# One ReLU moves from ScalarE to VectorE in a fused cluster attention and MLP kernel

## The chip, the cores and the metric

The kernel runs on one core of a Trainium2 chip. The metric is the device time of one execution in microseconds (us). A core has five engines that run their own instruction queues in order and wait for each other by semaphores: TensorE (PE in the profile, its weight loads are PEld), VectorE (DVE), ScalarE (ACT), GpSimd (POOL) and SyncE (SP), which here only issues transfers. Matmul results land in PSUM; everything else lives in SBUF.

## The reference

Queries, keys and values have shape (4 batches, 8 heads, 768 positions, 64). Each query and key is put into one of 16 clusters, a query attends to the keys of its own cluster, and the result (3072 tokens of 512) goes through an MLP with an inner layer of 2048:

```python
q_assign = np.argmax(np.einsum('bhsd,hcd->bhsc', q_n, c_n), axis=-1)
k_assign = np.argmax(np.einsum('bhsd,hcd->bhsc', k_n, c_n), axis=-1)
mask = q_assign[:, :, :, None] == k_assign[:, :, None, :]
scores = np.where(mask, scale * np.matmul(q, k.transpose(0, 1, 3, 2)), -1000000000.0)
attn = softmax(scores)            # max taken off, 1e-9 added to the sum
x = (attn @ v).transpose(0, 2, 1, 3).reshape(3072, 512)
h = x @ w_in
r = np.maximum(h, 0.0)
g = s * (r * r) + b
out = g @ w_out
```

## The kernel before

Products are taken in float16 with a high and a low part of each operand, so that three matmuls stand for one.

**Attention.** A *unit* is one (batch, query chunk, head pair, query tile of 128, head); there are 192. Query chunks are two tiles, 256 positions. For a unit, PE makes the scores `sc` (128 x 768, L456), DVE takes the row maximum (L465, `ssm`), ACT turns it into a bias (L472) and takes the exponential out of PSUM (L475, `p`), ACT writes the float16 high part `ph` (L119, in a few units DVE, L121), POOL the low part (L498), a transposing DMA turns both (L500, `PT`), and PE multiplies by the values into `px` (L517 to L519). DVE scales the result into `xs` (L525, L526, L529), and for each four units it is split, turned and put down as `x` (L540 to L546). Scores have two PSUM buffers.

**MLP.** A *step* is one (batch, query chunk, block `ft` of 128 inner columns); there are 12 x 16 = 192, named `r_b_c_ft`, `h_b_c_ft` and `g_b_c_ft` for batch, chunk and block. A step makes `h` (128 x 256 in one PSUM bank, 12 matmuls, L575), then takes the ReLU times a factor `cf` out of PSUM into `r` (L582), squares `r` into the float16 high part `g` (L584) and in place (L585), POOL subtracts the two for the low part of `g` (L590), and PE adds the step to the output sums `acc` (6 matmuls, L602). `cf` is one number per partition, made on DVE from the largest absolute value of the chunk's `x` (L560 to L564). There is one `h` bank (`ps_h`, bufs=1), so the `h` matmuls of a step wait until the ReLU of the step before has read it. `r` has two buffers, `g` four.

**Preparation.** For each batch and chunk, Q, K and V are loaded (L85, from SyncE's queue, behind the last transpose issued before), DVE takes their largest absolute value (L101: `amb_q`, `amb_k`, `vm`), PE and DVE spread it over the partitions (L97, L98), ACT and DVE split into high and low parts (L185, L187), and the cluster one-hot is made (L288 to L294). The weights are read once, narrowed ahead of the first step (L203 to L223), and split (L267, L269) while the first steps run.

**Order.** The main loop runs over units; step `m` is written `LAG` = 21 units behind. One pass writes scores, the output of step `m - 2`, the maximum and exponential, then `mlp_in` and `mlp_relu` of step `m`, then the low parts, values and one piece of each preparation at work. This is only a priority: the framework's scheduler then places each instruction on its engine's queue by its own estimate of times, so that a change of one instruction's engine can move others on all queues. On the chip each queue runs in the order so fixed.

## Time and profile before

| what | value |
|---|---|
| median of 3 runs | 986.11 us (985.94 to 988.25) |
| profiled execution | span 986.0 us, from its first to its last instruction |
| mean granted TensorE clock | 0.941 of full |
| PE / PEld busy | 834.3 us (85%) / 580.2 us (59%) |
| ACT busy | 726.4 us (74%), 1416 instructions |
| DVE busy | 673.0 us (68%), 1475 instructions |
| POOL busy | 550.2 us (56%) |
| the ReLU, L582 on ACT | 192 instructions, 89.1 us busy, 464 ns each |
| first and last ReLU | start at 179.0 and 977.8 us |

Only the span is given for the profiled execution, no time of its own beside it; it lies within the range of the runs. Busy time is a sum over stages with different limits; PE's busy time includes pipelining, so it says less than what PE waits for. In rows of groups the columns are: line, engine, operation, output and inputs with shapes, count, then total busy us, mean ns of one, then the engine's idle time just before them and what ended it. In rows of the timeline: start in us, duration in us, engine, line, operation, tiles, and in brackets the idle time before it and its releaser. In rows of waits: who waited, for whom, total us, number of times, the longest.

### The profile page before, as it was taken

The page shows a single profiled execution, that of the slowest core. Times are in us where ns is not written, and L with a number is a line of the kernel's source. Part 1 is how long each engine was busy: PE and PEld are TensorE (multiplying, and loading weights), DVE is VectorE, ACT ScalarE, POOL GpSimd, SP SyncE. Part 2 cuts the span into 40 slices and gives each one's busy share as a digit, 9 for nine tenths or more (in the row PEclk, how much of TensorE's full clock was granted, in tenths as well). Part 3 has the DMA queues.
Part 4 walks back from the last instruction along what each step waited for, and adds up shares of the span by engine and source line. Part 5 has one row for each costly group of instructions (what it writes and reads, how often), then busy time and mean ns, then how long its engine had stood idle before and what let it go on. Part 6 is the DMA issues. An engine that isn't in the chain of part 4 may idle for free. (4 is left out here: it accounts for less than half of the span.)

```text
span 986.0 us, 22497 instructions
## 1 busy us (share of the span) xinstructions
PE 834.3 (85%) x8625; PEld 580.2 (59%) x8625; DVE 673.0 (68%) x1475; ACT 726.4 (74%) x1416; POOL 550.2 (56%) x543
## 2 busy tenths in 40 slices
PE   0568524887899999998799999997889999999997
PEld 0347312654566666765566666765666666767764
DVE  7798889989687665658787756578867567473100
ACT  4476776877578788867678877876788977789443
POOL 3125755556456576655467656655566766667322
PEclk9955566999999999999999999999999999999999
DMA  6865883687678775698888767797888676777200
GB/s 181 204 196 158 222 210 90 138 194 134 128 144 163 156 161 123 140 210 154 171 164 156 169 132 156 138 203 181 138 160 173 151 119 142 142 138 149 44 23 21
DMA packets 450299, 147.36 MB, mean 149 GB/s; under 512 B 417936, under 2 KB 446608, under 8 KB 450192
## 3 DMA queue, kind: packets, MB, share of 16 engines
q1 hardware_dynamic: 450192, 145.93, 69.7%
q8 instruction: 67, 1.10, 0.5%
q14 instruction: 40, 0.33, 0.1%
HBM read 35.69 MB, written 6.29 MB: 43 GB/s over the span
## 5 line engine op out<-in xcount | busy, mean ns | idle before, releaser
L498 POOL TENSOR_TENSOR ph<-p,ph 128x768 f16<-128x768 f32 x184 | 308.6, 1677 | 170.7 <-ACT ph L119 135.8
L575 PE MATMUL h<-x,wis 128*128 128x256 f16 x2304 | 292.0, 275 | 17.3 <-ACT r L582 12.2
L602 PE MATMUL acc<-wos,g 128*128 128x512 f16 x1152 | 295.4, 380 | 4.7 <-POOL g L590 2.9
L575 PEld LDWEIGHTS <-wis 128*128 128x128 f16 x2304 | 223.1, 98 | 74.9 <-issue 16.6
L590 POOL TENSOR_TENSOR g<-r,g 128x256 f16<-128x256 f32 x192 | 133.3, 695 | 139.7 <-ACT r L585 129.8
L465 DVE TENSOR_REDUCE ssm<-sc 128x1 f32<-128x768 f32 x192 | 180.9, 950 | 16.2 <-PE sc L456 16.0
L475 ACT ACTIVATE p<-sc,ssm,qsm 128x768 f32<-128x768 f32 x192 | 188.1, 980 | 3.9 <-DMA PT<-ph 1.8
L602 PEld LDWEIGHTS <-g 128*128 128x128 f16 x1152 | 104.1, 98 | 88.2 <-POOL g L590 6.9
L119 ACT ACTIVATE ph<-p 128x768 f16<-128x768 f32 x174 | 144.8, 832 | 11.1 <-DMA PT<-ph 10.8
L472 ACT ACTIVATE ssm<-ssm,lift,qsm 128x1 f32<-128x1 f32 x192 | 73.4, 382 | 101.9 <-DVE ssm L465 101.4
L517 PE MATMUL px<-vh,PT 128*128 128x65 f16 x1104 | 119.9, 196 | 14.5 <-DVE ksm L98 5.2
L582 ACT ACTIVATE r<-h,cf 128x256 f32<-128x256 f32 x192 | 89.1, 464 | 55.0 <-PE h L575 50.8
L518 PE MATMUL px<-vl,PT 128*128 128x64 f16 x1104 | 119.9, 193 | 0.0
L519 PE MATMUL px<-vh,PT 128*128 128x65 f16 x1104 | 119.9, 194 | 0.0
L456 PE MATMUL sc<-KA,QA 128*128 128x384 f16 x384 | 101.1, 343 | 20.2 <-ACT p L475 16.9
L518 PEld LDWEIGHTS <-PT 128*128 128x128 f16 x1104 | 103.6, 100 | 21.2 <-issue 12.8
L517 PEld LDWEIGHTS <-PT 128*128 128x128 f16 x1104 | 103.9, 98 | 17.5 <-issue 9.1
L456 PE MATMUL sc<-KB,QB 128*128 128x384 f16 x384 | 100.2, 345 | 7.8 <-DMA QB<-qb 7.7
L519 PEld LDWEIGHTS <-PT 128*128 128x128 f16 x1104 | 103.6, 98 | 3.0
L584 ACT ACTIVATE g<-r 128x256 f16<-128x256 f32 x192 | 79.5, 414 | 3.8
L585 ACT ACTIVATE r<-r 128x256 f32<-128x256 f32 x192 | 79.1, 412 | 3.3
L525 DVE TENSOR_SCALAR ssm<-px 128x2 f32<-128x2 f32 x92 | 14.2, 155 | 88.3 <-PE px L519 88.2
(153 smaller groups left out, 1090.9 us busy)
## 6 DMA issues: line engine op xcount, KB each, us to landing
wst<-in_moe_w_in_dram SPq DMA_DIRECT2D x16, 512.0 KB, 4.5
wst<-in_moe_w_out_dram SPq DMA_DIRECT2D x16, 512.0 KB, 4.1
kn<-in_k_dram SPq DMA_DIRECT2D x16, 384.0 KB, 3.9
qn<-in_q_dram SPq DMA_DIRECT2D x24, 256.0 KB, 3.8
vn<-in_v_dram SPq DMA_DIRECT2D x16, 384.0 KB, 4.4
out_dram<-o SPq DMA_DIRECT2D x12, 512.0 KB, 3.2
PT<-ph SPq DMA_TRANSPOSE x184, 3.4
x<-xn SPq DMA_TRANSPOSE x48, 2.5
```

Of the source, the lines that this page charges most:

```text
L119: A.activation(dst, src, AF.Copy)
L456: last_score[0] = nc.tensor.matmul(sc[:, e, :HALF], X[:, col, :], y[:, h * S + e * HALF : h * S + (e + 1) * HALF], start=st, stop=not st)
L465: last_max[0] = V.tensor_reduce(SM[i // 4][:, 0, j : j + 1], U[i]["sc"], axis=AX.XY, op=ALU.max, negate=True)
L475: last_exp[0] = A.activation(p.rearrange("p (a b) -> p a b", a=2), u["sc"], AF.Exp, bias=bi, scale=u["scale"], **total)
L498: G.tensor_tensor(u["ph"][:, 1, :], u["p"], u["ph"][:, 0, :], op=ALU.subtract)
L517: nc.tensor.matmul(o1, PT[:, kt, :], vh[:, h, kt, : D + 1], start=(kt == 0), stop=False)
L518: nc.tensor.matmul(o, PT[:, kt, :], vl[:, h, kt, :], start=False, stop=False)
L519: nc.tensor.matmul(o1, PT[:, T + kt, :], vh[:, h, kt, : D + 1], start=False, stop=(kt == T - 1))
L575: nc.tensor.matmul(ph[:, :CW], WSP[ft][0][:, wl, kt, :], XS[(b, c, kt)][:, :, xl, :], start=(i == 0), stop=(i == len(terms) - 1))
L582: A.activation(r, ph[:, :CW], AF.Relu, scale=MS[(b, c)][0])
L590: G.tensor_tensor(g[:, 1, :], r, g[:, 0, :], op=ALU.subtract)
L602: nc.tensor.matmul(acc[:, t, :], g[:, gl, rows], WSP[ft][1][:, wl, :], start=(ft == 0 and gl + wl == 0), stop=(ft == NF - 1 and gl == 1))
```

## The change

The ReLU with its factor leaves ACT and becomes one VectorE instruction with two scalars: first the maximum of `h` and 0, then the product with `cf`. `cf` is positive, so that max(h, 0) x cf is what ACT computed as max(cf x h, 0). Both squares stay on ACT.

```diff
@@ -579,7 +579,7 @@
         n = f"{b}_{c}_{ft}"
         ph = GS[(b, c, ft)]
         r = sb.tile([P, CW], F32, tag="r", name=f"r_{n}", bufs=2)
-        A.activation(r, ph[:, :CW], AF.Relu, scale=MS[(b, c)][0])
+        V.tensor_scalar(r, ph[:, :CW], 0.0, MS[(b, c)][0], op0=ALU.max, op1=ALU.mult)
         g = sb.tile([P, 2, CW], F16, tag="g", name=f"g_{n}", bufs=4)
         A.activation(g[:, 0, :], r, AF.Square)
         A.activation(r, r, AF.Square)
```

The scheduler places the rest anew from the first ReLU on. DVE's queue around the preparation of the queries `qn_2_1_0` (batch 2, chunk 1, first four heads), which falls into the first steps of batch 1, chunk 2, before the change:

```order
L465 TENSOR_REDUCE ssm_100_7675<-sc_103_7870 128x1
L525 TENSOR_SCALAR ssm_96_7406<-px_96_7779 128x2
L465 TENSOR_REDUCE ssm_104_7970<-sc_104_7957 128x1
L526 RECIPROCAL ssm_96_7406<-ssm_96_7406 128x2
L529 TENSOR_TENSOR xs_24_7818<-px_96_7779,ssm_96_7406 128x128
L101 TENSOR_REDUCE amb_q2_1_0_7951<-qn_2_1_0_7868 128x2
L525 TENSOR_SCALAR ssm_96_7406<-px_98_7910 128x2
L526 RECIPROCAL ssm_96_7406<-ssm_96_7406 128x2
L529 TENSOR_TENSOR xs_24_7818<-px_98_7910,ssm_96_7406 128x128
```

The same place of DVE's queue with the change:

```order
L529 TENSOR_TENSOR xs_24_7818<-px_96_7779,ssm_96_7406 128x128
L582 TENSOR_SCALAR r_1_2_0_7770<-h_1_2_0_7757,cf_1_2_7753 128x256
L566 SCALAR_TENSOR_TENSOR xm_20_6746<-xm_20_6746,glob_130 128x1
L101 TENSOR_REDUCE amb_q2_1_0_7951<-qn_2_1_0_7868 128x2
L582 TENSOR_SCALAR r_1_2_1_7859<-h_1_2_1_7846,cf_1_2_7753 128x256
L525 TENSOR_SCALAR ssm_96_7406<-px_98_7910 128x2
L526 RECIPROCAL ssm_96_7406<-ssm_96_7406 128x2
L465 TENSOR_REDUCE ssm_104_7970<-sc_105_8004 128x1
```

The ReLU of step 0 of that chunk now stands ahead of the reduction over the loaded queries (L101), the ReLU of step 1 directly behind it.

ACT's queue in the same steps, before the change:

```order
L475 ACTIVATE p_102_7844<-sc_102_7825,ssm_100_7675,qsm_2_0_0_6743 128x768
L582 ACTIVATE r_1_2_0_7770<-h_1_2_0_7757,cf_1_2_7753 128x256
L584 ACTIVATE g_1_2_0_7772<-r_1_2_0_7770 128x256
L585 ACTIVATE r_1_2_0_7770<-r_1_2_0_7770 128x256
L472 ACTIVATE ssm_100_7675<-ssm_100_7675,lift_132,qsm_2_0_0_6743 128x1
L472 ACTIVATE ssm_104_7970<-ssm_104_7970,lift_132,qsm_2_0_1_7387 128x1
L582 ACTIVATE r_1_2_1_7859<-h_1_2_1_7846,cf_1_2_7753 128x256
L584 ACTIVATE g_1_2_1_7861<-r_1_2_1_7859 128x256
```

and with it:

```order
L475 ACTIVATE p_103_7886<-sc_103_7870,ssm_100_7675,qsm_2_0_0_6743 128x768
L472 ACTIVATE ssm_104_7970<-ssm_104_7970,lift_132,qsm_2_0_1_7387 128x1
L584 ACTIVATE g_1_2_0_7772<-r_1_2_0_7770 128x256
L585 ACTIVATE r_1_2_0_7770<-r_1_2_0_7770 128x256
L119 ACTIVATE ph_103_7968<-p_103_7886 128x768
L475 ACTIVATE p_104_7973<-sc_104_7957,ssm_104_7970,qsm_2_0_1_7387 128x768
L584 ACTIVATE g_1_2_1_7861<-r_1_2_1_7859 128x256
L585 ACTIVATE r_1_2_1_7859<-r_1_2_1_7859 128x256
```

The two ReLUs are gone, and the squares of a step now stand one exponential later than before (behind that of unit 103 instead of 102).

Two other places of DVE's queue with the change, both in the last batch's preparation: the keys of head pair 3 (`kn_3_3`) in step 5 of batch 2, chunk 1, and then the second half of the queries of chunk 0 in step 11.

```order
L525 TENSOR_SCALAR ssm_132_9955<-px_132_10396 128x2
L101 TENSOR_REDUCE amb_k3_3_10451<-kn_3_3_10355 128x1
L526 RECIPROCAL ssm_132_9955<-ssm_132_9955 128x2
L529 TENSOR_TENSOR xs_33_10435<-px_132_10396,ssm_132_9955 128x128
L582 TENSOR_SCALAR r_2_1_5_10483<-h_2_1_5_10470,cf_2_1_10043 128x256
```

```order
L294 TENSOR_SCALAR kb_131<-oo_k3_3_10851 128x12x64
L101 TENSOR_REDUCE amb_q3_0_1_10941<-qn_3_0_1_10854 128x2
L525 TENSOR_SCALAR ssm_136_10316<-px_138_10895 128x2
L465 TENSOR_REDUCE ssm_144_10959<-sc_144_10946 128x1
L526 RECIPROCAL ssm_136_10316<-ssm_136_10316 128x2
L582 TENSOR_SCALAR r_2_1_11_10977<-h_2_1_11_10964,cf_2_1_10043 128x256
```

In both a ReLU now stands a few rows behind a reduction over a load; before the change DVE's queue held no ReLU at these places.

## The prediction

> **What bounds the kernel now.** I read the page's first two parts, then the stretches of the span, the groups of instructions, the waits, and last the timeline at single places.

> ```profile
> span 986.0 us, 22497 instructions
> PE 834.3 (85%) x8625; PEld 580.2 (59%) x8625; DVE 673.0 (68%) x1475; ACT 726.4 (74%) x1416; POOL 550.2 (56%) x543
> ```

> No engine is full, so the stretches decide. Columns: start and end, length, then busy time and instruction count of PE, PEld, DVE, ACT and POOL, PE's granted clock, DMA share, GB/s.

> ```profile
> 200.00:250.00 50.00, 39.10 (x386) 24.73 (x384) 45.54 (x96) 37.56 (x70) 30.05 (x25) 0.95 0.82 165
> 300.00:430.00 130.00, 125.43 (x1369) 88.55 (x1368) 83.49 (x187) 108.11 (x213) 85.39 (x80) 0.99 0.71 150
> 430.00:520.00 90.00, 77.77 (x888) 54.57 (x886) 70.82 (x159) 65.24 (x126) 50.21 (x50) 1.00 0.88 177
> 520.00:640.00 120.00, 115.07 (x1254) 80.27 (x1252) 75.02 (x170) 99.59 (x196) 77.98 (x74) 1.00 0.76 148
> 640.00:720.00 80.00, 70.36 (x818) 49.94 (x815) 64.07 (x149) 59.02 (x114) 44.32 (x46) 1.00 0.85 172
> 720.00:915.00 195.00, 186.81 (x2055) 131.20 (x2054) 119.70 (x261) 159.71 (x314) 127.69 (x118) 1.00 0.72 147
> 915.00:986.00 71.00, 65.31 (x502) 43.75 (x499) 6.25 (x21) 32.00 (x74) 17.44 (x26) 0.98 0.09 24
> ```

> There are three kinds. In the light ones (300 to 430, 520 to 640, 720 to 915) PE is busy 96% and idles 4.6 + 4.9 + 8.2 = 17.7 us together. In the dense ones, where the next batch's K, Q and V are prepared (430 to 520, 640 to 720) or weights are still being split (200 to 250), PE idles 12.2 + 9.6 + 10.9 = 32.7 us, and there DVE is busier (79%, 80%, 91%) than ACT (72%, 74%, 75%). Behind 915 the scores are done and PE has only MLP matmuls left: I expect no gain or loss there. So PE sets the time, and what a change on ACT and DVE can move is the PE idle time of 200 to 915, 50.4 us at most downwards.

> Who makes PE wait, and who makes DVE and ACT wait, from 178 us, where the first ReLU is near (total us, times, longest):

> ```profile
> ACT r L582 <- PE h L575: 50.8, 45, 5.1
> DVE amb_q L101 <- DMA qn<-in_q_dram: 38.7, 16, 4.9
> PE h L575 <- ACT r L582: 12.2, 10, 3.1
> DVE amb_k L101 <- DMA kn<-in_k_dram: 10.2, 7, 2.1
> DVE vm L101 <- DMA vn<-in_v_dram: 9.6, 7, 2.8
> PE sc L456 <- ACT p L475: 8.3, 8, 1.8
> ```

> ACT lateness costs PE 12.2 + 8.3 = 20.5 us. But the two longest of it do not begin on ACT:

> ```profile
> 475.18 0.38 PE L575 MATMUL h<-x,wis 128*128 128x256 f16 x2 [3.05 <-ACT r L582]
> 474.38 0.39 ACT L472 ACTIVATE ssm<-ssm,lift,qsm 128x1 f32<-128x1 f32 x1 [3.63 <-DVE ssm L465]
> 474.67 0.46 ACT L582 ACTIVATE r<-h,cf 128x256 f32<-128x256 f32 x1
> ...
> 683.41 0.27 PE L575 MATMUL h<-x,wis 128*128 128x256 f16 x1 [3.12 <-ACT r L582]
> 682.61 0.39 ACT L472 ACTIVATE ssm<-ssm,lift,qsm 128x1 f32<-128x1 f32 x1 [3.67 <-DVE ssm L465]
> ```

> Each time ACT had idled 3.6 us for a row maximum that DVE computed late, and the ReLU stood behind it. Without these two, 20.5 - 6.2 = 14.3 us begin on ACT.

> The three rows with DMA are the ones that matter: DVE stands still 38.7 + 10.2 + 9.6 = 58.5 us for a load of Q, K or V whose largest absolute value it must take, and all that is queued behind on DVE stands too. Today the ReLU is not in that queue.

> **The change part by part.** *Removed:* 192 activations from ACT. *Added:* 192 tensor_scalars on DVE; the built order has all 192 on DVE and none on ACT, so the change does what it says.

> ```profile
> L582 ACT ACTIVATE r<-h,cf 128x256 f32<-128x256 f32 x192 | 89.1, 464 | 55.0 <-PE h L575 50.8 <-DVE xm L565 1.9 <-POOL g L590 0.8
> L280 DVE TENSOR_SCALAR bias<-pb,glob x1: 750/750/750, 267.8 to 267.8; 128x512 f32<-128x512 f32 x1
> L289 DVE TENSOR_TENSOR oe_q<-pq,om_q x24: 274/292/293, 29.9 to 878.0; 128x128 f32<-128x128 f32 x24
> L98 DVE TENSOR_REDUCE qsm<-am_q x24: 408/418/425, 10.1 to 862.4; 128x2 f32<-128x256 f32 x24
> ```

> The new operation has no row of its own. The nearest is L280, the same operation out of PSUM with a scalar per partition, 750 ns for twice the elements: the upper bound. L98 reads the same 256 columns of PSUM in 418 ns without that scalar: the lower bound. Between L289 (128 columns, 292) and L280 (512, 750) a straight line gives 292 + 128 x 458/384 = 445 ns; I take 0.45 us. So ACT loses 89.1 us and DVE gains 192 x 0.45 = 86.4: DVE becomes the busier of the two, 759 against 637. For one ReLU alone 0.45 stands against 0.464; that difference is nothing, and PE waits for either through the single h bank. The two squares and the subtraction behind it keep their engines.

> [...]

> *Term A, the ReLU behind a load.* In the new order of DVE a ReLU often stands directly behind one of those reductions. Three places hurt, by the trace's times. At the first, DVE today:

> ```profile
> 547.01 0.29 DVE L529 TENSOR_TENSOR xs<-px,ssm 128x128 f32<-128x128 f32 x1
> 552.22 0.69 DVE L101 TENSOR_REDUCE amb_q<-qn 128x2 bf16<-128x512 f32 x1 [4.92 <-DMA qn<-in_q_dram]
> 547.16 0.46 ACT L582 ACTIVATE r<-h,cf 128x256 f32<-128x256 f32 x1
> 550.01 0.48 ACT L582 ACTIVATE r<-h,cf 128x256 f32<-128x256 f32 x1
> 548.44 1.47 PE L575 MATMUL h<-x,wis 128*128 128x256 f16 x12
> ```

> DVE waits from 547.3 to 552.22, ACT meanwhile does two ReLUs and PE two groups of h. In the new order r_1_2_1 (the one of 547.16) stands directly behind amb_q2_1_0 (the one of 552.22): it would end at 552.22 + 0.69 + 0.45 = 553.36, and the h group of 548.44 starts then: 4.9 us later. The other two:

> ```profile
> 704.69 0.95 DVE L101 TENSOR_REDUCE amb_k<-kn 128x1 bf16<-128x768 f32 x1 [1.66 <-DMA kn<-in_k_dram]
> 699.87 0.46 ACT L582 ACTIVATE r<-h,cf 128x256 f32<-128x256 f32 x1
> 701.87 0.82 PE L575 MATMUL h<-x,wis 128*128 128x256 f16 x6
> ...
> 730.84 0.69 DVE L101 TENSOR_REDUCE amb_q<-qn 128x2 bf16<-128x512 f32 x1 [3.86 <-DMA qn<-in_q_dram]
> 726.06 0.47 ACT L582 ACTIVATE r<-h,cf 128x256 f32<-128x256 f32 x1 [0.54 <-PE h L575]
> 729.86 1.36 PE L575 MATMUL h<-x,wis 128*128 128x256 f16 x11
> ...
> L465 DVE TENSOR_REDUCE ssm<-sc 128x1 f32<-128x768 f32 x192 | 180.9, 950 | 16.2 <-PE sc L456 16.0
> L525 DVE TENSOR_SCALAR ssm<-px 128x2 f32<-128x2 f32 x92 | 14.2, 155 | 88.3 <-PE px L519 88.2
> ```

> r_2_1_5 (699.87) now stands behind amb_k3_3 (704.69) with a reciprocal and an xs row between (0.15 by L525, a row as small, and 0.29): 704.69 + 0.95 + 0.4 + 0.45 = 706.5 against 701.87, 4.6 us. r_2_1_11 (726.06) stands behind amb_q3_0_1 (730.84) with a row maximum and two small rows between (0.95 + 2 x 0.155, less the overlap of their starts: about 1.1 us): 730.84 + 0.69 + 1.1 + 0.45 = 733.1 against 729.86, 3.2 us. Together 12.7 us. Not all of it reaches the end: PE idles in this part anyway, and a PE that comes later waits less for what it waited for before. I take two thirds: **+8.5** (bounds 0 and 12.7; nothing if the loads land earlier because ACT now feeds the transposes ahead of them sooner).

> *Term B, DVE full.* In the dense stretches DVE gets 8, 20 and 18 ReLUs (the same stretches with the instructions of L582 alone):

> ```profile
> 200.00:250.00 50.00, 3.70 (x8) 0.95 0.82 165
> 430.00:520.00 90.00, 9.24 (x20) 1.00 0.88 177
> 640.00:720.00 80.00, 8.33 (x18) 1.00 0.85 172
> ```

> That is 46 x 0.45 = 20.7 us, which puts DVE at 49.1 of 50, 79.8 of 90 and 72.2 of 80. Row maxima, preparations and ReLUs queue behind each other where PE already waits. Of this work I let a quarter reach PE, **+5.2** (bounds 0 and 20.7), since idle slots remain in two of the three stretches. In the light stretches DVE goes from 62% to an estimated 72%, 0.45 us for each ReLU in some 4 us, and hides it.

> *Term C, relief on ACT.* Of the 14.3 us of PE idle time that begin on ACT, 40% go: **-5.7** (bounds 0 and -14.3). ACT waited 50.8 us for h with exponentials queued behind; these go ahead now, but their row maxima stand on DVE, which takes over that wait, so most of it only changes queues.

> Sum: 986.0 + 8.5 + 5.2 - 5.7 = 994.0. The span stands 0.1 us below the runs' median of 986.11, so the number serves for both.

> **The rivals.**

> *Faster, ACT's relief wins.* If loads land before DVE comes to them, A is nothing, and C comes in full: 986.0 + 5.2 - 14.3 = 977. For it: ACT is the busier engine in the light stretches (108.11 against 83.49 of 130). Against: ACT there mostly waits for DVE's maxima, and PE idles only 17.7 us in all of them. It decides if fewer than two of the three h groups are pushed.

> *No change.* PE's own slack takes most: A at a third (4.2), B at half (2.6), C as taken: 986.0 + 4.2 + 2.6 - 5.7 = 987.

> *DVE becomes the bound* in the dense stretches: A and B in full, no C: 986.0 + 12.7 + 20.7 = 1019. For it: 49.1 of 50 in the first of them; against: 200 to 250 alone is that full.

> [...]

> **How the numbers follow.** The forecast gets 0.50, the faster rival 0.24, no change 0.15, the full DVE 0.08, the cheap ReLU 0.03. A measurement tells about 0.3% from no change, here 3 us. The cheap case, 990, lies near that limit and is put with no change: faster 0.24, same 0.18, slower 0.58. For 8 in 10 the range leaves out half of the faster case and the full DVE: 980 to 1010; the forecast's own range is 988 to 1003.

> **What would show it.** Right: L582 on DVE at 0.42 to 0.50 us; a row in which PE's h waits for DVE's r, well above the 12.2 us of today, with its long waits (over 2 us) right behind an L101 that waits for DMA; ACT near 637 and DVE near 759 us; the tail behind 915 unchanged, PE at full there. Term B shows in DVE's busy time at 430 to 520 and 640 to 720 over 88% with more PE idle time there. Wrong: h waits for r no longer than now and scores no longer wait for p, which is the faster rival; or the DVE waits for loads shrink well below 58.5 us, and term A with them.

## The result and the profile after

The change costs time: 998.18 us (median of 4 runs, 996.43 to 1000.15) against 986.66 us for the kernel before on the same chip (985.94 to 988.25). The ratio on record is 1.0107, 95% interval [1.0083, 1.0131]: 10.6 us, with 8.2 to 12.9 us in the interval. It is not the quotient of the two medians, which would be 1.0117 (11.5 us); the ratio with its interval is used from here on.

The first lines of the changed kernel's page, and the ReLU's group (its columns as before):

```profile
span 996.1 us, 22681 instructions
PE 839.3 (84%) x8625; PEld 582.3 (58%) x8625; DVE 744.4 (75%) x1667; ACT 659.3 (66%) x1224; POOL 553.6 (56%) x543
```

```profile
L582 DVE TENSOR_SCALAR r<-h,cf 128x256 f32<-128x256 f32 x192 | 92.0, 479 | 122.0 <-PE h L575 98.7 <-PE px L519 15.9 <-POOL xn L543 3.1
```

Two things are to be seen. The ReLU takes 479 ns on DVE where it took 464 on ACT, as good as the same. And PE does the same 8625 matmuls in 839.3 instead of 834.3 us of busy time: of the 10.1 us by which the span grew, 5.0 are matmuls that ran longer and 5.1 are idle time. The matmuls that ran longer are a thing of the clock (from the first ReLU to the tail its half-clock stretches cost 10.7 us in this profile and 5.0 in that of before, by the count of the last section); more profiles show below that their share isn't tied to the change.

The waits of the changed kernel from 178 us on, chosen rows (who waited, for whom: total us, times, longest):

```profile
ACT g L584 <- DVE r L582: 139.1, 108, 7.3
DVE r L582 <- PE h L575: 98.7, 66, 3.7
ACT ssm L472 <- DVE ssm L465: 65.5, 68, 3.9
DVE amb_q L101 <- DMA qn<-in_q_dram: 24.4, 15, 3.4
PE h L575 <- DVE r L582: 14.1, 16, 2.4
DVE amb_k L101 <- DMA kn<-in_k_dram: 8.9, 9, 2.2
DVE vm L101 <- DMA vn<-in_v_dram: 7.7, 6, 2.8
PE sc L456 <- ACT p L475: 3.5, 6, 1.0
```

DVE now stands before ReLUs whose `h` is not there yet (98.7 us), ACT stands before squares (139.1 us). The waits for loads have shrunk from 58.5 to 24.4 + 8.9 + 7.7 = 41.0 us: DVE is later at them, so that the data are there. PE waits for the ReLU 14.1 us where it was 12.2, and for the exponential 3.5 where it was 8.3.

The stretches of the changed kernel, with the bounds of those shown of before (columns as there):

```profile
200.00:250.00 50.00, 40.27 (x408) 26.08 (x407) 48.79 (x99) 35.59 (x67) 29.63 (x25) 1.00 0.75 163
300.00:430.00 130.00, 122.19 (x1355) 85.99 (x1352) 99.60 (x216) 95.55 (x176) 82.34 (x78) 0.97 0.70 148
430.00:520.00 90.00, 79.18 (x869) 54.16 (x867) 73.28 (x178) 59.05 (x109) 52.85 (x52) 0.98 0.91 176
520.00:640.00 120.00, 115.22 (x1253) 81.02 (x1252) 84.90 (x195) 87.89 (x165) 77.39 (x72) 0.99 0.74 146
640.00:720.00 80.00, 70.50 (x747) 48.37 (x743) 64.63 (x158) 50.95 (x92) 44.33 (x42) 0.98 0.83 177
720.00:915.00 195.00, 186.51 (x2045) 131.42 (x2044) 138.32 (x312) 145.81 (x267) 124.20 (x116) 0.99 0.73 144
```

In the dense stretches (200, 430 and 640) PE idles 9.7 + 10.8 + 9.5 = 30.0 us, no more than the 32.7 of before; in the light ones 7.8 + 4.8 + 8.5 = 21.1 against 17.7. Together that is only 0.7 us more. The stretch from 250 to 300, which the prediction's table leaves out, holds the largest part of the 5.1 us: PE idles 6.1 us there against 2.2. Its row before, then after:

```profile
250.00:300.00 50.00, 47.77 (x468) 31.38 (x467) 35.58 (x76) 33.37 (x65) 23.50 (x25) 0.98 0.77 135
250.00:300.00 50.00, 43.91 (x427) 28.73 (x426) 38.66 (x91) 25.97 (x49) 24.42 (x23) 0.97 0.66 140
```

DVE is busy 77% in it, less than in any of the dense stretches (98%, 81%, 81%). So in this pair the loss is not where DVE is fullest. The bounds are fixed times, though, and the work behind them has shifted (by 4 to 8 us at the three places below), so a stretch doesn't hold quite the same work in both kernels.

**The three places of the prediction, after.** DVE and PE around the queries `qn_2_1_0`, the keys `kn_3_3` and the queries `qn_3_0_1` (timeline, columns as before; 714.07 has no wait in brackets):

```profile
555.82 2.11 PE L575 MATMUL h<-x,wis 128*128 128x256 f16 x12
556.39 0.69 DVE L101 TENSOR_REDUCE amb_q<-qn 128x2 bf16<-128x512 f32 x1 [1.86 <-DMA qn<-in_q_dram]
558.04 0.48 DVE L582 TENSOR_SCALAR r<-h,cf 128x256 f32<-128x256 f32 x1 [0.96 <-PE h L575]
...
711.90 0.96 DVE L101 TENSOR_REDUCE amb_k<-kn 128x1 bf16<-128x768 f32 x1 [2.24 <-DMA kn<-in_k_dram]
713.24 0.48 DVE L582 TENSOR_SCALAR r<-h,cf 128x256 f32<-128x256 f32 x1
714.07 1.47 PE L575 MATMUL h<-x,wis 128*128 128x256 f16 x12
...
738.96 0.69 DVE L101 TENSOR_REDUCE amb_q<-qn 128x2 bf16<-128x512 f32 x1 [2.45 <-DMA qn<-in_q_dram]
740.57 0.47 DVE L582 TENSOR_SCALAR r<-h,cf 128x256 f32<-128x256 f32 x1
741.09 1.14 PE L575 MATMUL h<-x,wis 128*128 128x256 f16 x9 [0.74 <-DVE r L582]
```

The ReLUs stand behind the loads just as the order said. But at the first place its own `h` was only done at 555.82 + 2.11 = 557.93, so nothing was pushed; at the second the next `h` began without a wait; at the third it waited 0.74 us. The prediction had 4.9, 4.6 and 3.2 us.

What the pushes look like instead, at one of the longest (DVE ahead of the ReLU of 764.62, and the `h` that waited for it):

```profile
761.04 0.75 DVE L610 SCALAR_TENSOR_TENSOR o<-acc,xm,bias 128x512 f32<-128x512 f32 x1
761.77 0.74 DVE L610 SCALAR_TENSOR_TENSOR o<-acc,xm,bias 128x512 f32<-128x512 f32 x1
762.43 0.95 DVE L465 TENSOR_REDUCE ssm<-sc 128x1 f32<-128x768 f32 x1
763.43 0.96 DVE L465 TENSOR_REDUCE ssm<-sc 128x1 f32<-128x768 f32 x1
764.62 0.48 DVE L582 TENSOR_SCALAR r<-h,cf 128x256 f32<-128x256 f32 x1
```

```profile
765.16 1.03 PE L575 MATMUL h<-x,wis 128*128 128x256 f16 x8 [1.76 <-DVE r L582]
```

The `h` for this ReLU had been done for 4.5 us. DVE did not stand still; it worked through two outputs and two row maxima first. For every wait of `h` for a ReLU in this trace I counted how much of the ReLU's lateness lay in a load that DVE waited for: 1.3 us of 15.2 in all (the count includes one wait ahead of 178 us). In the four other kernels below with every ReLU on DVE and no early filler the same count gives 3.6 to 6.0 us of 17.9 to 22.2. The rest stands behind DVE's other work.

### The profile page after: what moved, and what is told of

Its sections match the earlier page's. It is cut to its first block, busy times and chain, and to the rows that moved or that the text cites. A ratio compares the mean times of both kernels' runs of the same rounds, so it can differ in the third digit from the quotient of the medians.

```text
span 996.1 us, 22681 instructions
## 1 busy us (share of the span) xinstructions
PE 839.3 (84%) x8625; PEld 582.3 (58%) x8625; DVE 744.4 (75%) x1667; ACT 659.3 (66%) x1224; POOL 553.6 (56%) x543
## 5 line engine op out<-in xcount | busy, mean ns | idle before, releaser
L575 PE MATMUL h<-x,wis 128*128 128x256 f16 x2304 | 294.8, 276 | 23.1 <-DVE r L582 15.2
L602 PE MATMUL acc<-wos,g 128*128 128x512 f16 x1152 | 299.0, 381 | 3.5 <-POOL g L590 3.3
L575 PEld LDWEIGHTS <-wis 128*128 128x128 f16 x2304 | 225.2, 99 | 88.0 <-issue 29.1
L590 POOL TENSOR_TENSOR g<-r,g 128x256 f16<-128x256 f32 x192 | 137.5, 717 | 159.5 <-ACT r L585 154.6
L475 ACT ACTIVATE p<-sc,ssm,qsm 128x768 f32<-128x768 f32 x192 | 188.1, 980 | 10.0 <-DMA PT<-ph 3.6
L465 DVE TENSOR_REDUCE ssm<-sc 128x1 f32<-128x768 f32 x192 | 181.6, 949 | 13.5 <-PE sc L456 12.3
L582 DVE TENSOR_SCALAR r<-h,cf 128x256 f32<-128x256 f32 x192 | 92.0, 479 | 122.0 <-PE h L575 98.7
L584 ACT ACTIVATE g<-r 128x256 f16<-128x256 f32 x192 | 79.0, 412 | 139.5 <-DVE r L582 139.1
L472 ACT ACTIVATE ssm<-ssm,lift,qsm 128x1 f32<-128x1 f32 x192 | 73.1, 381 | 78.2 <-DVE ssm L465 76.8
L519 PE MATMUL px<-vh,PT 128*128 128x65 f16 x1104 | 119.3, 195 | 0.0
L456 PE MATMUL sc<-KA,QA 128*128 128x384 f16 x384 | 101.2, 344 | 16.5 <-ACT p L475 13.4
L456 PE MATMUL sc<-KB,QB 128*128 128x384 f16 x384 | 100.9, 343 | 8.6 <-DMA QB<-qb 8.6
L519 PEld LDWEIGHTS <-PT 128*128 128x128 f16 x1104 | 104.3, 99 | 3.0 <-issue 0.3
L585 ACT ACTIVATE r<-r 128x256 f32<-128x256 f32 x192 | 79.1, 412 | 10.6 <-ACT g L584 0.7
L456 PEld LDWEIGHTS <-QB 128*128 128x128 f16 x384 | 38.5, 102 | 37.8 <-DMA QB<-qb 11.9
```

The source lines that it names most:

```text
L456: last_score[0] = nc.tensor.matmul(sc[:, e, :HALF], X[:, col, :], y[:, h * S + e * HALF : h * S + (e + 1) * HALF], start=st, stop=not st)
L465: last_max[0] = V.tensor_reduce(SM[i // 4][:, 0, j : j + 1], U[i]["sc"], axis=AX.XY, op=ALU.max, negate=True)
L475: last_exp[0] = A.activation(p.rearrange("p (a b) -> p a b", a=2), u["sc"], AF.Exp, bias=bi, scale=u["scale"], **total)
L519: nc.tensor.matmul(o1, PT[:, T + kt, :], vh[:, h, kt, : D + 1], start=False, stop=(kt == T - 1))
L575: nc.tensor.matmul(ph[:, :CW], WSP[ft][0][:, wl, kt, :], XS[(b, c, kt)][:, :, xl, :], start=(i == 0), stop=(i == len(terms) - 1))
L582: V.tensor_scalar(r, ph[:, :CW], 0.0, MS[(b, c)][0], op0=ALU.max, op1=ALU.mult)
```

## The experiments

All ratios are against the kernel before on the same chip, with a 95% interval. Every edit also lets the scheduler place all queues anew, so that each run differs from its partner in more than its edit; none of the runs holds the order fixed. The fillers of the first and third group compute numbers that nothing uses; they add work and leave none out. All other kernels compute everything, on other engines or at other times.

**An idle load on either engine.** A reduction on DVE added to each step of the kernel before; a copy on ACT added to each step of the changed kernel.

```diff
+    idle = const([P, 320], F32, "idle")        # e1_load and e2_act
...
         A.activation(r, ph[:, :CW], AF.Relu, scale=MS[(b, c)][0])
+        V.tensor_reduce(spare, idle[:, :320], axis=AX.X, op=ALU.max)        # e1_load
...
         V.tensor_scalar(r, ph[:, :CW], 0.0, MS[(b, c)][0], op0=ALU.max, op1=ALU.mult)
+        A.activation(idle[:, :256], idle[:, :256], AF.Copy)        # e2_act
```

> The ReLU stays on ACT as before; DVE gets one more reduction per step (128x320 from SBUF, an estimated 0.48 us by L101's 410 ns for 256 columns), which reads a constant and waits for no matmul. It adds the same busy time to DVE as the change, and takes nothing off ACT. If a fuller DVE alone costs time (the prediction's term B, 5.2 us, and no relief on ACT): 990 to 998 us. If the cost is that DVE now waits for h and holds its other work back (98.7 us of such waits in the profile after): within 3 us of 986.

> The ReLU on DVE as in the change; ACT gets one copy per step (128x256 in SBUF, an estimated 0.41 us by L585), which waits for nothing, so ACT is not relieved. If the relief on ACT is worth what the prediction took (term C, 5.7 us): 1002 to 1006. If the relief is worth nothing: within 3 us of 998.

Measured: 1047.64 us, 1.059 [1.0541, 1.064], and 1013.36 us, 1.0245 [1.0209, 1.0281]. Neither is near either of its expectations, and neither tells anything on the theories. The filler depends on nothing, and the scheduler drew it ahead. Busy time of the filler (L586) of the first kernel on DVE, of the second on ACT, before and behind 178 us:

```profile
0.00:178.00 178.00, 54.91 (x116) 0.71 0.67 168
178.00:975.00 797.00, 35.97 (x76) 0.96 0.79 145
```

```profile
0.00:178.00 178.00, 48.10 (x116) 0.71 0.75 182
178.00:975.00 797.00, 31.29 (x77) 0.98 0.77 144
```

116 of the 192 ran while the weights were still being read. These runs price a load on the start.

**Loads three passes earlier,** with and without the change; the reductions stay where they were.

```diff
+    AHEAD = 3
...
         yield                      # in prep_q, behind the load; in prep_k alike
+        if b + c:
+            for _ in range(AHEAD):
+                yield
...
-                    at(s0, prep_q(b, c, hq))
+                    at(s0 - AHEAD, prep_q(b, c, hq))
...
-                at(48 * b - 20 + 4 * hp, prep_k(b, hp))
+                at(48 * b - 20 + 4 * hp - AHEAD, prep_k(b, hp))
```

> The kernel before, with the loads of Q and K (behind the first ones) issued three passes earlier and their reductions where they were, so that DVE stands less for loads (58.5 us of such waits before). Control for the next. If DVE's stalls behind loads cost little while the ReLU is on ACT: 982 to 987. If they cost as much either way: below 980.

> The changed kernel with the same earlier loads. By the prediction's term A (ReLU behind a load, 8.5 us) it gains 6 to 9 us on 998, and clearly more than the control gains on 986: 989 to 992. If term A is not what costs, it gains what the control gains and no more, and stays some 12 us above it.

Measured: 988.2 us, 0.9993 [0.9966, 1.002], and 991.72 us, 1.0042 [1.002, 1.0065]. The change costs 1.0042/0.9993 = 0.5% on top of earlier loads, instead of 1.07%; 6.5 us of its loss are gone. The control gained nothing, and the second time lies in the range that term A gave (989 to 992). But the waits of the second kernel speak against term A (its line numbers are one higher near 102 and seven higher in the MLP):

```profile
DVE amb_q L102 <- DMA qn<-in_q_dram: 18.9, 15, 2.5
PE h L582 <- DVE r L589: 18.3, 22, 2.8
DVE vm L102 <- DMA vn<-in_v_dram: 12.4, 9, 3.3
DVE amb_k L102 <- DMA kn<-in_k_dram: 10.6, 7, 4.2
```

DVE waits for loads 18.9 + 12.4 + 10.6 = 41.9 us, as long as without the edit (41.0), and PE waits longer for the ReLU, not shorter; by the count above 5.1 us of that lie behind loads, where it was 1.3. What was won is not the stall at the loads. The half-clock loss is smaller in this trace (5.4 us against 10.7, worked out as in the last section), but one profile doesn't make that a cause. It stays open.

**The loads on the engines again,** with a filler that can't run early, since it reads the square `g` of two steps before.

```diff
+        if len(kept) > 1:
+            V.tensor_reduce(spare, kept[-2][:, 0, :], axis=AX.X, op=ALU.max)      # e1b_load: before + this
+            A.activation(spent, kept[-2][:, 0, :], AF.Copy)                       # e2b_act: after + this
         g = sb.tile([P, 2, CW], F16, tag="g", name=f"g_{n}", bufs=4)
         A.activation(g[:, 0, :], r, AF.Square)
         A.activation(r, r, AF.Square)
+        kept.append(g)
```

> As the first filler run, but the DVE filler (a reduction of 128x256 in float16, an estimated 0.41 us) reads the g of two steps earlier, so that it can't run ahead of its step. ReLU on ACT. DVE gets 190 x 0.41 = 78 us in the steps where the change puts 92. If DVE's fullness is what the change costs (term B, with no relief on ACT): 992 to 1000. If it is the ReLU's own place in DVE's queue (it waits for h, and h's bank waits for it): within 3 us of the kernel before.

> The changed kernel with a filler on ACT (a copy of 128x256, an estimated 0.41 us) that reads the g of two steps earlier: ACT is not relieved. Term C says the relief is worth 5.7 us: 1.5% to 1.8% above the kernel before, some 1003. If relief is worth nothing: about 1.1% above, as the change. If it is worth more than the prediction gave it: over 1.8%.

Measured: 1013.22 us, 1.0229 [1.0196, 1.0262], and 1010.03 us, 1.0201 [1.0172, 1.023]. The first is dearer than both of its expectations; the second falls under the last of its three, relief worth more than the prediction gave it. The fillers' groups, first on DVE, then on ACT, and of the first kernel the group of POOL that shares `g` with it:

```profile
L588 DVE TENSOR_REDUCE spare<-g 128x1 f32<-128x256 f16 x190 | 78.5, 413 | 100.6 <-ACT g L590 100.0
L597 POOL TENSOR_TENSOR g<-r,g 128x256 f16<-128x256 f32 x192 | 133.0, 693 | 127.0 <-ACT r L591 96.2 <-DVE spare L588 25.2 <-PE acc L609 4.6
```

```profile
L588 ACT ACTIVATE spent<-g 128x256 f32<-128x256 f16 x190 | 76.2, 401 | 0.0
```

The ACT filler waits for nothing (0.0 us of idle time in front of it). It puts 715.1 - 659.3 = 55.8 us of the 67.1 us that ACT lost back on it, and costs 1.0201/1.0107 = 0.9%, some 9 us (the two intervals taken together: 5 to 13). So ACT's relief was worth about that much, as far as a copy stands for a ReLU. And with ACT nearly as loaded as before, the ReLU on DVE costs the whole 2.0%. The DVE filler is no pure load: DVE waits 100.0 us for `g` in front of it, and POOL 25.2 us for it. It is an operation of about the ReLU's length, with waits of its own in DVE's queue, and it costs about what the ReLU on DVE costs, 2.3% against 2.0%. That PE waits for the ReLU itself, and not for the filler, shows in no dearer price. The filler's cost shows elsewhere: PE's scores wait 14.3 us for the turned queries `QB` where they waited 5.8 before, and 10.4 us for the exponential where it was 8.3.

**The change in one part of the steps only.** The dense steps are 0 to 27 and 7 to 27 of the next two batches' 48, 70 in all; the light ones are the other 122.

```diff
-        A.activation(r, ph[:, :CW], AF.Relu, scale=MS[(b, c)][0])
+        m = steps.index((b, c, ft))
+        dense = m < 144 and (m < 28 or 7 <= m % 48 < 28)
+        if dense:                     # e4_dense; in e4_light the two branches are exchanged
+            V.tensor_scalar(r, ph[:, :CW], 0.0, MS[(b, c)][0], op0=ALU.max, op1=ALU.mult)
+        else:
+            A.activation(r, ph[:, :CW], AF.Relu, scale=MS[(b, c)][0])
```

> The ReLU on DVE only in the 70 steps that run beside weight splits or beside the next batch's K and V (steps 0 to 27, and 55 to 75 and 103 to 123); the other 122 stay on ACT. By the prediction (B falls in these stretches, and two of A's three places at 704 and 730 us): most of the loss, 0.6% to 1.1%. By a cost per ReLU that is the same everywhere: 70 of the 168 ahead of the tail, 0.4%.

> The complement: 122 steps on DVE (24 of them in the tail), the 70 dense ones on ACT. By the prediction only A's place at 547 us costs here (4.9 us of push), and relief on ACT works against it: -0.3% to +0.2%. By a cost per ReLU that is the same everywhere: 98 of 168, 0.6%.

Measured: 993.75 us, 1.0039 [1.0025, 1.0053], and 998.01 us, 1.0092 [1.0066, 1.0118]. Together 1.3%, about the whole (1.07%). Per ReLU that is 0.39% of 989.67 us over 70, 55 ns, in the dense steps and 0.92% over 122, 75 ns, in the light ones (93 ns over the 98 ahead of the tail), with intervals that overlap. The dense steps came out at the even cost (0.4%) and below what the prediction gave them; the light ones lie above both of their expectations (0.2% and 0.6%). The light stretches hide nothing, and the dense ones are not dearer.

**Work taken off DVE.** The low parts of Q (and in a second pair of kernels of K and V) are subtracted on POOL instead of DVE; the branch for it is in the kernel, for the first chunk. It has a price: ACT scales the operand in an operation of its own.

```diff
-            both.append(split(qb[:, hs, :, 0, :], qa[:, hs, :, 0, :], qn[:, hs], sm[:, 2, j : j + 1], b + c == 0))
+            both.append(split(qb[:, hs, :, 0, :], qa[:, hs, :, 0, :], qn[:, hs], sm[:, 2, j : j + 1], True))
...
-        yield from split(ka[:, :, :, 0, :], ka[:, :, :, 1, :], kn, sm[2], False)
+        yield from split(ka[:, :, :, 0, :], ka[:, :, :, 1, :], kn, sm[2], b > 0)      # K and V: e5_qkv and e5_after alone
...
-            yield from split(vh[:, :, :, :D], vl, vns[hp], vm[:, 7:8], False)
+            yield from split(vh[:, :, :, :D], vl, vns[hp], vm[:, 7:8], b > 0)
```

Q, K and V, on the changed kernel and on the kernel before, and Q alone on the kernel before:

> The changed kernel (ReLU on DVE), with other work taken off DVE: the low part of Q, K and V behind the first batch's is subtracted on POOL instead of DVE (44 operations of 989 ns, 24 of about 1180: 72 us of DVE busy time less, against 92 that the ReLU brought), for which ACT scales once more (an estimated 38 us) and POOL gains an estimated 70 us. If DVE's load is the cost (the tied filler: 22.6 us for 78 us of load), some 20 us come back and ACT's extra 38 us cost 4 to 5 (9 us for 78 by the other filler): 980 to 986, or -0.8% to -0.2%. If the ReLU's place in DVE's queue is the cost, or POOL now holds PE up: no better than +0.7%.

> The kernel before with Q's, K's and V's low parts on POOL: 72 us less on DVE, an estimated 38 more on ACT, 70 more on POOL. By the fillers' prices: -21 + 4.5 = -16 us, 970 to 978 (-1.2% to -1.9%). If POOL (56% busy before) becomes the bound: no better than the run with Q alone, or slower than before.

> The kernel before (ReLU on ACT) with only Q's low parts moved to POOL: 42 us less on DVE, an estimated 18 more on ACT, 31 more on POOL. By the fillers' prices: -12 + 2 = -10 us, 977 to 981 (-1.0%). If DVE's load only costs when it is added on top: within 0.3% of the kernel before.

Measured, in this order: 998.66 us, 1.0098 [1.006, 1.0136]; 990.45 us, 1.0032 [1.0001, 1.0063]; 977.08 us, 0.988 [0.982, 0.9941]. The first misses its first expectation (980 to 986): DVE has 51 us less to do than in the changed kernel (693.1 against 744.4) and no time is won. The second misses its own (970 to 978) and ends as its last clause has it, slower than Q alone. The third is as expected and beats both kernels. It leaves the ReLU on ACT. Its page:

```profile
span 974.5 us, 22561 instructions
PE 834.4 (86%) x8625; PEld 580.4 (60%) x8625; DVE 633.1 (65%) x1431; ACT 738.4 (76%) x1460; POOL 577.3 (59%) x587
```

44 subtractions have gone from DVE to POOL and 44 scalings have come to ACT. That K and V on top of Q cost 1.5% again (1.0032/0.988) isn't explained by these runs; POOL is the engine that got their work. In the two profiles PE waits 16.1 us for `pk`, the products of the keys with the cluster centres, where it waited 7.3 with Q alone, and the keys' subtraction takes 1646 ns on POOL where it took 1223 on DVE. That points at the chain of the keys, but no run tests it.

**The square closed:** Q's low parts on POOL, with the ReLU on DVE.

```diff
-            both.append(split(qb[:, hs, :, 0, :], qa[:, hs, :, 0, :], qn[:, hs], sm[:, 2, j : j + 1], b + c == 0))
+            both.append(split(qb[:, hs, :, 0, :], qa[:, hs, :, 0, :], qn[:, hs], sm[:, 2, j : j + 1], True))      # on the changed kernel
```

> The changed kernel with Q's low parts on POOL alone, the partner of the run that did this to the kernel before (0.988). It closes the square of ReLU on ACT or DVE by Q's low parts on DVE or POOL. If the change costs what it does because DVE has too much to do in the way of PE, the ReLU costs clearly less here, where some 40 us of DVE's work are gone: 0.3 to 0.6% above 0.988, a ratio of 0.991 to 0.994 (980 to 984 us). If the cost belongs to the ReLU's own place (its turn in DVE's queue, the buffers r and h, the clock after PE's pauses), however full DVE is, it stays at 1.0 to 1.2%: 0.998 to 1.000 (987 to 990 us).

Measured: 988.32 us, 1.0005 [0.9988, 1.0022]. The square of ratios:

| | Q's low parts on DVE | on POOL | what POOL brings |
|---|---|---|---|
| ReLU on ACT | 1 | 0.988 | -1.2% |
| ReLU on DVE | 1.0107 | 1.0005 | -1.0% |
| what the change costs | +1.07% | +1.27% | |

With some 40 us less of DVE's work in its way (744.4 to 703.7) the ReLU costs as much as before, 1.27% with an uncertainty of some 0.65%. That DVE's work costs only where DVE is too full (0.3 to 0.6%) doesn't fit this, but 0.6% is at the edge of the interval. The pair with K and V on POOL too, where DVE has 51 us less, lies between: 1.0098/1.0032, 0.66% with an uncertainty of some 0.5%. So a price that falls somewhat with DVE's load isn't excluded. The other expectation has the number, but not alone: a fixed price for each us that DVE gets to do, at whatever load, gives a square without a product term too. It fits three sides. Q's low parts give back 11.9 us for 39.9 us of DVE's busy time (673.0 to 633.1), 0.30 us for one; with the ReLU on DVE 10.1 for 40.7, 0.25; and the ReLU, with ACT loaded again, costs 19.9 us for 742.0 - 673.0 = 69.0 us, 0.29. (Q's part includes what its scalings cost on ACT.) On ACT one us is worth 9.2/55.8 = 0.16 by the filler, 0.10 to 0.23 with its interval; Q's first figure alone reaches from 0.15 to 0.45. K and V fit no such price, nor does the DVE filler, 22.7 us for 720.1 - 673.0 = 47.1 us, 0.48.

Where the ReLU's part is lost, a row of the waits shows, in the kernel with Q on POOL and the ReLU on ACT, and then with the ReLU on DVE:

```profile
PE h L575 <- ACT r L582: 3.4, 7, 1.0
```

```profile
PE h L575 <- DVE r L582: 20.4, 22, 2.2
```

The same row of all profiles that can be paired, from 178 us on (total us, times):

| kernel | ReLU on ACT | ReLU on DVE |
|---|---|---|
| as it is | 12.2, 10 | 14.1, 16 |
| loads earlier | 5.2, 10 | 18.3, 22 |
| Q on POOL | 3.4, 7 | 20.4, 22 |
| Q, K, V on POOL | 9.9, 10 | 21.3, 24 |
| with a filler (on DVE, on ACT) | 7.6, 12 | 16.7, 21 |
| mean | 7.7 | 18.2 |

In each line PE waits longer for a ReLU on DVE, by 10.5 us in the mean. The last line is no clean pair, since its two fillers load different engines; without it the mean is 10.9 us. That is near what the change costs, but line by line the two don't go together: the waits of the four pairs grow by 1.9, 13.1, 17.0 and 11.4 us, the times by some 10.6, 4.8, 12.4 and 6.5 us by the ratios. All waits of PE from 178 us on, summed, grow by 3.0, 8.0, 12.8 and 9.6 us, in three of the four pairs by less than the row of `h` alone. The 12.2 us of the kernel before are the largest of their column: the two waits of 3.1 us that the prediction showed are half of it. So the pair before and after shows the effect at its smallest, and by itself would hide it.

## Why the prediction was right, and where it was wrong

The direction and the size were right: forecast 994.0 us with an own range of 988 to 1003, measured 998.18. The sum held although its terms were off in both directions, and that is partly luck: by the estimates below A was some 7 us too high, B some 13 us too low, and C gave back some 3.5 us too little.

- **The price of the ReLU** was right: 0.479 us for 0.45 taken. The cheap ReLU, to which the chances give 0.03 at 990 us, is shown by no run: the ReLU took 479 ns on DVE and 464 on ACT.
- **Term A, the ReLU behind a load** (+8.5 us), is the step that failed. The mechanism is there (waits of `h` behind a load come to 1.3 us after, and by the same count to 6.0 us with Q on POOL), but the three pushes of 4.9, 4.6 and 3.2 us came out as 0, 0 and 0.7. The step took the landing time of the loads and the end of `h` from the old trace and moved only the ReLU. In the new run everything ahead was some microseconds later, the loads were waited for 41.0 instead of 58.5 us, and `h` and the load met at another phase.
- **Term B, DVE full** (+5.2 us, a quarter of the work in the dense stretches, nothing in the light ones), had the mechanism but too small, and in the wrong place. The experiment in parts puts 3.9 us on the 70 dense steps and 9.1 us on the 122 light ones. DVE reached 81% in the two later dense stretches (73.28 of 90, 64.63 of 80), not 88%, and PE idled there no more than before. "62% to 72%, and hides it" was the wrong sentence: the ReLU of 764.62 stood behind two row maxima of 0.95 and 0.96 us in a stretch in which DVE was busy 71% (138.32 of 195), and `h` waited 1.76 us for it.
- **Term C, relief on ACT** (-5.7 us), was too small: about -9 us by the ACT filler, inside its bounds. A and B together are then what the ReLU costs with ACT nearly as loaded as before, some 2.0% or 20 us, instead of 13.7; with the load waits of 1.3 us for A, some 18.6 are left for B, close to its upper bound of 20.7.
- **Not in the sum**: matmuls at half clock behind PE's pauses, the 5.0 us of longer busy time. They show no tie to the change. By the count of the last section the five profiles of the table with the ReLU on ACT lose 5.0 to 11.2 us so, 8.9 in the mean, those with it on DVE 5.4 to 13.3, 8.7 in the mean; the profile of before is the luckiest of its column. What grows is PE's idle time: from the first ReLU to the last score by 4.6 us in the pair before and after (53.1 to 57.7), and by 7.5, 11.6 and 10.3 us in the pairs with earlier loads, with Q and with Q, K and V on POOL.
- **The idle time that can move**: 50.4 us leaves out the stretch from 250 to 300 (2.2 us), which is where most of the idle time of the change came in.
- **Signs.** ACT was to be near 637 and DVE near 759; they are at 659.3 and 744.4. The error was to add group sums: 89.1 us taken from ACT's groups lowered its busy time by 67.1, and 92.0 brought to DVE raised it by 71.4, since instructions that follow each other overlap at their ends (DVE's 1667 in the profile of after are 819.0 us long one by one and 744.4 us as busy time). The row of `h` waiting for the ReLU rose from 12.2 to only 14.1, not well above it, and the long waits behind loads didn't appear. One sign against the forecast did, the shrinking waits for loads, and the time still went the forecast way: the sign was tied to term A alone.
- **Rivals.** The faster one was to win if fewer than two of the three groups were pushed. Only one was, by 0.7 us, and the kernel was slower all the same: that rival left out that DVE's plain work pushes the ReLU as well. DVE as the bound (1019) didn't come either: with 40 us less of its work the cost stayed, within the uncertainty given, as it was. No change (987) lies outside the measured interval.

What is shown: PE waits longer for a ReLU on DVE in five of five lines of the table, mostly behind DVE's work and not behind loads (1.3 to 6.0 us of 15.2 to 22.2 are loads); the cost doesn't fall when DVE has 40 us less to do, within the uncertainty given; a load of ACT's size put back on ACT costs about half of what the ReLU then costs on DVE. What is only argued is the reason: DVE's row maxima feed ACT and through it PE, so that each operation more in its queue delays two chains, at any load. A rival that no run tests is the new order of all queues: the squares stand one exponential later on ACT, and no kernel moved the ReLU with the rest of the order held. That the change costs time in all four pairs, with 1.07%, 0.5%, 1.27% and 0.66%, each with an order of its own, speaks against chance in one order, but not against an order that comes with the ReLU's new engine. What stays open as well: what the earlier loads gave back, and why K and V on POOL cost time.

## What to carry to other kernels

Of two engines about as full, one can be dearer than the other: here a us of work cost 0.25 to 0.30 us of time on DVE (65 to 75% busy) and 0.16 on ACT (66 to 71% busy), as estimates whose intervals overlap in part. So a move between engines is priced by measuring each end with a small load in the loop, and not by which of the two is fuller. A push read from the old trace at one place is good for the sign, not for the size, because the change shifts the phase of everything behind it (here 12.7 us read at three places and 0.7 measured, in work that came 4 to 8 us later); count that kind of wait over the whole run, and in more than one profile. What paid here was Q's low parts on POOL, 1.2%; K's and V's low parts on top of them took it back, so that such a move is to be measured and not assumed.

## What the runs showed of the hardware

**In these traces the granted clock changes in steps of 3.413 us.** In the changed kernel's trace, PE waits 3.63 us at `pk` (released by DVE, L64) and then runs at half clock (granted clock 0.50 in the last row below). PE's rows, then the two stretches around them:

```profile
692.67 0.17 PE L338 MATMUL pk<-cT,KA 128*128 128x16 f16 x1 [3.63 <-DVE xm L64]
693.48 2.57 PE L575 MATMUL h<-x,wis 128*128 128x256 f16 x12
```

```profile
690.25:693.67 3.42, 0.94 (x26) 0.88 (x27) 2.68 (x11) 0.21 (x1) 0.00 (x0) 1.00 1.16 298
693.67:697.08 3.41, 3.41 (x16) 2.10 (x15) 3.24 (x7) 2.23 (x4) 2.48 (x2) 0.50 1.19 164
```

Twelve matmuls of `h` take 2.57 us there and 1.47 elsewhere. A pause nearly as long in the kernel before, the 3.05 us ahead of 475.18 that the prediction quotes, cost nothing more: the twelve matmuls behind it took 1.47 us. Its two windows on the same kind of grid:

```profile
470.58:473.99 3.41, 1.55 (x18) 0.97 (x15) 3.41 (x8) 0.17 (x1) 0.98 (x1) 1.00 1.49 207
473.99:477.41 3.42, 2.23 (x34) 1.85 (x34) 1.84 (x7) 2.25 (x6) 0.67 (x1) 1.00 0.82 248
```

What it costs: at a granted 0.50 one such window of 3.413 us does an estimated 1.7 us of full-clock work less, half its length. From the first ReLU to the tail that is 5.0 us in the profile of before and 10.7 in that of after (for each pair of matmuls in such a stretch, the distance above that at full clock; how that is averaged moves the figure by up to 1 us).

**A filler's price is more than its length.** The two fillers have groups of 76.2 us (ACT) and 78.5 us (DVE), and cost 9 and 23 us. In front of the second DVE waits 100.0 us, and POOL waits 25.2 us for it; so only the first comes near a clean price of load.
